# Turning a segment's result on VectorE instead of TensorE, with the weights' rows dealt out by eights, and three edits around it

## The chip, the cores and the metric

The kernel runs on one core of one Trainium2 chip. The metric is the device time of one execution in microseconds (us); lower is better. Engines are named as in the profile: PE (TensorE; PEld its weight loads), DVE (VectorE), ACT (ScalarE), POOL (GpSimd), SP (SyncE, which here only issues DMAs). ACTq, POOLq and SPq are the issues of DMAs on those engines.

## What is computed

Two independent heads whose outputs stand side by side.

Head A is attention with a recurrent memory. x is [2048, 1024], cut into 64 segments of 32 rows; the memory has 8 rows; there are 32 heads of width 128, and all weights are bf16:

```python
mem = mem0
for s in range(64):
    h = concatenate([mem, x[32*s:32*s+32]])          # 40 rows of 1024
    q, k, v = h @ Wq, h @ Wk, h @ Wv                 # 1024 -> 32 heads x 128
    p = softmax(mask(q @ k.T * 128**-0.5))
    o = (p @ v) @ Wo                                 # 4096 -> 1024
    mem = o[:8]                                      # goes into the next segment
    out_a[32*s:32*s+32] = o[8:]
```

The memory rows make the 64 segments a chain: no segment's projections can be finished before the result of the one before is there.

Head B is a long convolution per channel: K[d, l] = Re(sum over n of C dt B exp(dt A l)) for 1024 channels, 128 states and 2048 steps, then y = irfft(rfft(u) rfft(K)) + u D.

## The kernel before

**Part B comes first** (`part_b`, up to about 700 us). It builds tables, computes the filter and its spectrum by matmuls with sine matrices (MF), and multiplies and transforms back. What part A can have ahead of time runs beside it: `Ahead.transposes` turns x (L107), `Ahead.projections` computes q, k and v of the last 8 rows of each segment for all segments (L167) and leaves them in DRAM as PKd (keys, queries) and VXd (values, and the turned x). The last stage of part B is a loop over 16 blocks b. In it `load_k` fetches rows of the filter (KT from Kd, L1008) by many small DMAs, collected in `keys` and sent ten per block; `load_inverse` fetches u into uu (L1247); `spectrum` and `inverses` are PE work; `pointwise` is DVE work; L1306 and L1307 multiply and add u on DVE; the result is stored from ACT's queue (L1308). `load_inverse` runs NIV = 3 inverses ahead in 2 x NIV = 6 buffers. In the same loop `resident` loads part A's weights (L229) on SyncE, in the order of the program, into space that part B gives up.

**Part A** (`part_a`) keeps most of the weights in SBUF as blocks of [128, 2048], keyed (matrix, half, kc): kc is one of the eight groups of 128 rows of the 1024, and group kc holds rows 128 kc to 128 kc + 127. Twelve blocks a segment have no place and are streamed from DRAM copies (WD_k, WD_q, WD_v, WD_o, 512 KB each) through four slots, wst w0 to w3 (L297, SyncE): a slot is loaded again once PE has used it. Three more blocks (`KEPT`) stay in PSUM as raw words: `load_kept` puts them there, and `fetch` copies them on DVE (L292) into the arena, a small area of SBUF with fixed offsets (`AT`), each time they are needed. Of two of them (`HALF`) one half stays in SBUF instead, loaded a second time from DRAM.

The instruction order of each engine is the order of the program (`manual_schedule`). A segment goes through: k of half 0 (`quads`, L365, eight blocks of four concurrent 32-column matmuls of 512), q of half 0, k of half 1; then `put_kl` (L379, POOL) copies the early keys from the tile pk, which `load_pk` fetched from PKd on ACT's queue (L327) at the end of the segment before; scores (L390, L394); q of half 1, v, softmax on DVE and ACT, p v (L444), and the output projection (`oproj`, L475) into pp[:, 1, :], a [128, 256] f32 tile in PSUM: partition 32 qt + r holds row r, columns 256 qt to 256 qt + 255.

Then the result is turned, since the next segment needs its memory rows as columns of hT [128, 8, 32] (row group on the partitions, then kc, then row). This is the end of a segment:

```python
for j in range(2):                                               # ACT, L568
    nc.scalar.copy(out=osb[:, 128*j:128*j+128], in_=pp[:, 1, 128*j:128*j+128])
pv_l(pl[:], 1, V1, L1)                                           # PE
for j in range(2): nc.tensor.transpose(out=pt_o[j], in_=osb[...])   # PE, L574
for j in range(2): nc.vector.tensor_copy(out=hT[:, :, XM:SL]..., in_=pt_o[j]...)  # DVE, L576
fetch(("k", 0, 7))                                               # DVE, L292, five pieces
nc.scalar.copy(out=ob[:, 1, 0:128], in_=pp[:, 0, 0:128])         # ACT, L579
pk = load_pk(s + 1)                                              # ACT's queue, L327
nc.scalar.copy(out=ob[:, 1, 128:256], in_=pl[:]...)              # ACT, L582
stores(s, ob)                                                    # ACT's queue, L343 and L347
```

The first copy of hT holds the even row groups, the second the odd ones, and so the next k of half 0 goes through the groups as 0, 2, 4, 6, 1, 3, 5, 7. Group 7 is the one that `fetch` unpacks. osb is ob[:, 0, :].

Of the kernel before, what the change touches and what calls it, by code (L numbers as in the profile page):

```python
# [10 lines left out]
BF16 = mybir.dt.bfloat16  # L11
F32 = mybir.dt.float32
# [20 lines left out]
SLOTS = 4  # L33
# [6 lines left out]


def weight_blocks(Wq, Wk, Wv, Wo):
    W3 = {"k": Wk.rearrange("(kc p) he -> kc p he", p=128),
          "q": Wq.rearrange("(kc p) he -> kc p he", p=128),
          "v": Wv.rearrange("(kc p) he -> kc p he", p=128)}
    WoU = Wo.rearrange("(u h e) d -> u e h d", h=2, e=128)

    def src(key):
        if isinstance(key, str):
            return W3[key]  # L50
        if key[0] == "o":
            return WoU[key[1]]
        m, t, kc = key
        return W3[m][kc][:, t * 2048:(t + 1) * 2048]
    return src
# [18 lines left out]
class Ahead:  # L74
# [18 lines left out]
    def transposes(self, pool, ps, ident):  # L93
        nc = self.nc
        def load(b):
            xb = pool.tile([128, self.Dm], BF16, name="xb", tag="xb")
            nc.gpsimd.dma_start(out=xb[:], in_=self.x[b * 128:(b + 1) * 128, :])
            return xb
        xbs = [load(b) for b in range(3)]
        yield  # L100
        for b in range(self.S // 128):
            if b + 3 < self.S // 128:
                xbs.append(load(b + 3))
            xb = xbs[b]
            pt = ps.tile([128, self.KC, 4, self.SL], BF16, name="pt_x", tag="ptx")
            for kc in range(self.KC):
                nc.tensor.transpose(out=pt[:, kc, :, :].rearrange("p a b -> p (a b)"), in_=xb[:, kc * 128:(kc + 1) * 128], identity=ident[:])  # L107
            yield
            xst = pool.tile([128, 4, self.KC, self.XM], BF16, name="xst", tag="xst")
            nc.scalar.copy(out=xst[:].rearrange("p s k r -> p k s r"), in_=pt[:, :, :, 0:self.XM])  # L110
            nc.scalar.copy(out=self.xTl[:, :, 4 * b:4 * b + 4, :], in_=pt[:, :, :, self.XM:self.SL])  # L111
            nc.sync.dma_start(out=self.VXd[4 * b:4 * b + 4, :, 256:].rearrange("s p f -> p s f"), in_=xst[:].rearrange("p s k r -> p s (k r)"))
            yield
# [119 lines left out]
def part_a(ctx, tc, x, src, WD, HE, seg_len, out_a, ahead, W_res, rest, places, first):  # L233
    nc = tc.nc
    S, Dm = x.shape
    M = 8
    SL = seg_len
    E = 128
    KC = Dm // 128
    NS = S // SL  # L240
    assert SL == 32 and M == 8 and Dm == 1024 and HE == 4096
    XM = 24
# [5 lines left out]
    ident, mask, BD, BDx, BDL, hT = ahead.consts  # L248
# [4 lines left out]
    wst = ahead.wst  # L253
    wres = ctx_w.enter_context(tc.tile_pool(name="a_wres", bufs=1, side="right"))

    loads = [SLOTS]
# [20 lines left out]
    ps = ctx_l.enter_context(tc.tile_pool(name="a_ps", bufs=1, space=PSUM))  # L277
    ps_k = ctx_l.enter_context(tc.tile_pool(name="a_keep", bufs=1, space=PSUM))
    kept, ahead_of, halves = {}, {}, {}
# [11 lines left out]
    def words(out, in_):  # L291
        nc.vector.tensor_scalar(out=out.bitcast(I32), in0=in_.bitcast(I32), scalar1=0, scalar2=None, op0=ALU.bitwise_or)  # L292

    def stage(key, in_):
        t_ = wst.tile([128, 2048], BF16, name="wst", tag="w%d" % (loads[0] % SLOTS))
        loads[0] += 1
        nc.sync.dma_start(out=t_[:].rearrange("e (h d) -> e h d", h=2) if len(in_.shape) == 3 else t_[:], in_=in_)  # L297
        return t_

    def load_kept(key):  # L300
        t_ = first.pop(key) if key in first else stage(key, src(key))
        kept[key] = {}
        for n in (1,) if key in HALF else (0, 1):
            kept[key][n] = ps_k.tile([128, 512], F32, name="keep", tag="keep%d" % sum(len(b) for b in kept.values()))
            words(kept[key][n][:], t_[:, 1024 * n:1024 * n + 1024])
        if key in HALF:
            t_ = ahead.low["half"] if key[0] == "q" else wres.tile([128, 1024], BF16, name="Whalf")
            nc.sync.dma_start(out=t_[:], in_=src(key)[:, 0, :] if key[0] == "o" else src(key)[:, 0:1024])
            halves[key] = [(0, 1024, t_)]

    def fetch(key):

# [44 lines left out]
    for s in range(NS):  # L357
        def quads(m, t, kcs, a=None):
            if a is None:
                a = ps.tile([128, 512], F32, name="acc", tag=BANK[m, t])  # L360
            for kc in kcs:
                w = unit((m, t, kc))
                for g in range(4):
                    for o_, rhs in columns(w, 512 * g, 512):
                        nc.tensor.matmul(a[32 * g:32 * g + 32, o_:o_ + rhs.shape[1]], lhsT=hT[:, kc, :], rhs=rhs,  # L365
                                         start=(kc == 0), stop=(kc == KC - 1), tile_position=(0, 32 * g), skip_group_check=True)
            return a
# [107 lines left out]
                            nc.tensor.matmul(po[32 * qt:32 * qt + 32, o_:o_ + rhs.shape[1]], lhsT=oT[:, h % 4, (h % 16) // 4, :], rhs=rhs,  # L475
                                             start=False, stop=(h == 31), tile_position=(0, 32 * qt), skip_group_check=True)

        a = quads("k", 0, (0, 2, 4, 6, 1, 3, 5, 7))
        k0 = evac(a, "k0")
        a = quads("q", 0, range(0, 6))  # L480
        fetch(("q", 0, 7))
# [82 lines left out]
        oproj(pp[:, 1, :], (8, 10, 12, 14, 9, 11, 13, 15), o1)  # L564
        ob = at("ob", 2, 256)
        osb = ob[:, 0, :]
        for j in range(2):
            nc.scalar.copy(out=osb[:, 128 * j:128 * j + 128], in_=pp[:, 1, 128 * j:128 * j + 128])  # L568
        pl = ps.tile([128, 4, 32], F32, name="pl", tag="b2")
        pv_l(pl[:], 1, V1, L1)  # L570
        if s + 1 < NS:
            pt_o = [ps.tile([128, 4, SL], BF16, name="tro", tag=tag) for tag in ("b0", "b1")]
            for j in range(2):
                nc.tensor.transpose(out=pt_o[j][:].rearrange("p a b -> p (a b)"), in_=osb[:, 128 * j:128 * j + 128], identity=ident[:])  # L574
            for j in range(2):
                nc.vector.tensor_copy(out=hT[:, :, XM:SL].rearrange("p (q j) r -> p j q r", j=2)[:, j], in_=pt_o[j][:, :, XM:SL])  # L576
        if s + 1 < NS:
            fetch(("k", 0, 7))
        nc.scalar.copy(out=ob[:, 1, 0:128], in_=pp[:, 0, 0:128])  # L579
# [67 lines left out]
def part_b(ctx, tc, u, A_re, A_im, B_re, B_im, C_re, C_im, log_dt, Dskip, out_b, ahead, copies, residents, first_state):  # L647
    nc = tc.nc
# [36 lines left out]
    with tc.tile_pool(name="b_par", bufs=1) as par, tc.tile_pool(name="b_parh", bufs=2) as parh, tc.tile_pool(name="b_mg", bufs=2) as mg, \  # L685
# [84 lines left out]
        o = 0  # L770
# [467 lines left out]
        for j, op in ((0, ALU.add), (1, ALU.subtract)):  # L1238
            v.tensor_tensor(out=Bt[:, kc, j], in0=Y[:, 0], in1=Y[:, 1], op=op)

    NIV = 3
    unsent = []

    def load_inverse(dq, c):
        r, mc = c // 4, c % 4
        uu = iv.tile([128, 2, DQ], BF16, name="uu", tag="uu", bufs=2 * NIV)
        sy.dma_start(out=uu[:], in_=u_v[r][:, mc:mc + 2, DQ * dq:DQ * dq + DQ])  # L1247
        return uu

# [70 lines left out]
    for b in range(16):  # L1320
        dq = b // 4
        if b % 4 == 0:
            Bs[dq] = (bp0, bp)[dq % 2].tile([128, 4, 2, 2, 2, DQ], BF16, name="Bt", tag="B")
        if b == 0:
            ks += [load_k(DQ * i, DQ, (sy,), KT2[i - 2], keys) for i in (2, 3)]
        if b == 3:
            nxt = [load_inverse(*todo[n_]) for n_ in range(NIV)]
            pointwise(b, *now)
            ctx_h.close()
            ctx_p.close()  # L1330
            ps_h = ctx.enter_context(tc.tile_pool(name="b_psh", bufs=3, space=PSUM))
            ps_y = ctx.enter_context(tc.tile_pool(name="b_psy", bufs=2, space=PSUM))
        if b + 1 < 16:
            s_ = [ps_h.tile([128, 2, 2, DQ], F32, name="hps", tag="h") for _ in range(2)]
            spectrum(b + 1, [halves(t_) for t_ in s_])
            then = s_[0][:], odd([halves(t_) for t_ in s_])
        if b != 3:
            pointwise(b, *now)
        now = then
        if b + 2 < 16:  # L1340
            spectra.append(load_u(b + 2))
        for _ in range(min(10, len(keys))):
            keys.pop(0)()
        if b < 4:
            for i in (2 * b, 2 * b + 1):
                sy.dma_start(out=MI[i][:], in_=MId[2 * i:2 * i + 2].rearrange("c p a k q -> p c a k q"))
        for _ in range({1: 1, 2: 1, 3: 1, 6: 4, 11: 2, 12: 2, 13: 4, 14: 4}.get(b, 0)):
            next(resident)
        if b == 4:
            state = first_state(iv.tile([8, D], BF16, name="m0", bufs=1), iv.tile([128, 8, 24], BF16, name="xt0", bufs=1))  # L1350
            next(state)
        if b == 13:
            state.send(ps_y.tile([128, 8, 128], BF16, name="yp", tag="yp")[:, :, 0:8])
        if b >= 4:
            inverses(2)
        if b == 6:
            negate(ks[1:])
# [38 lines left out]
def kernel(  # L1396
# [78 lines left out]
    def first_state(m0, xt):  # L1475
        nc = tc.nc
        hT = constants(tc, ahead)
        nc.sync.dma_start(out=xt[:].rearrange("p k r -> p (k r)"), in_=ahead.VXd[0, :, 256:])
        nc.sync.dma_start(out=m0[:], in_=A_mem0[0])
        pm = yield  # L1480
        for kc in range(8):
            nc.tensor.transpose(out=pm[:, kc, :], in_=m0[:, kc * 128:(kc + 1) * 128], identity=ahead.consts[0][0:8, 0:8])
        nc.vector.tensor_copy(out=hT[:, :, ahead.XM:], in_=pm)
        nc.gpsimd.tensor_copy(out=hT[:, :, 0:ahead.XM], in_=xt[:])
        yield
# [40 lines left out]
```

## Time and profile before

| | |
|---|---|
| median of 3 runs | 2073.23 us (2067.98 to 2073.27) |
| the profiled execution | 2060.34 us, of which the span from first to last instruction is 2058.6 |
| mean granted PE clock | 0.982 |
| part A, first to last of 64 segments | L579 runs from 749.0 to 1998.7 us |
| last matmuls of part A (L611) | from 1998.55 us, 55 us |
| DMA | 590.78 MB, 287 GB/s on the mean |
| streamed blocks | 256 + 192 + 192 + 128 = 768 DMAs of 512 KB |

How to read it: PE's busy time is modelled for pipelined matmuls. A "wait" line gives who waited, for what, the total in us, how often, and the longest. A timeline line gives the start and length in us, the engine, the line of the kernel, the operation, output and input, and in brackets the idle time of the engine before it with what ended it. In the chain of waits each row is what the end waited on at that time. In the 40 slices each digit is a busy share in tenths of 51.5 us.

### The profile page before, as it was taken

To read this page: it belongs to the slowest core of one execution; us is meant where nothing else is said; L and a number is where in the kernel's file an instruction comes from. 1 tells how busy PE (TensorE), PEld (TensorE's weight loads), DVE (VectorE), ACT (ScalarE), POOL (GpSimd) and SP (SyncE) were. 2 spreads that over 40 slices of the span, in tenths; PEclk is the share of its full clock that TensorE was granted. 3 is DMA by queue.
4 is the path that set the end of the run, shared out by engine and by line. 5 is a ranking of instruction groups with operands and counts; after the bars stand their busy time and mean duration, and the time that the engine had idled before them with its cause. 6 is when DMAs were issued, how large, how long until landed. Compare 5 with 4: busy or idle time off the path is not lost.

```text
span 2058.6 us, 78592 instructions
## 1 busy us (share of the span) xinstructions
PE 1875.7 (91%) x33734; PEld 1190.4 (58%) x33734; DVE 1416.1 (69%) x3352; ACT 1051.5 (51%) x1981; POOL 379.8 (18%) x748
## 2 busy tenths in 40 slices
PE   2699999977999779999999999999999999999999
PEld 1365666656888535555555555555555555555554
DVE  8689989989899346666656656666566666666650
ACT  5899999961333234444444444444444444444430
POOL 2133343353000011111111111111111111111121
PEclk9999999989999879999999999999999999999999
DMA  7697986565736899999999999999999999999991
GB/s 192 177 255 213 261 229 180 157 207 184 228 123 206 311 330 340 341 342 344 344 334 340 340 339 339 347 333 334 338 340 354 344 343 347 339 331 350 333 341 52
DMA packets 351186, 590.78 MB, mean 287 GB/s; under 512 B 108536, under 2 KB 228376, under 8 KB 348788
## 3 DMA queue, kind: packets, MB, share of 16 engines
q1 hardware_dynamic: 297016, 528.00, 75.6%
q10 hardware_dynamic: 44812, 28.26, 4.4%
q0 software_dynamic: 9008, 29.49, 4.3%
q8 instruction: 264, 4.33, 0.8%
q14 instruction: 86, 0.70, 0.1%
HBM read 530.86 MB, written 65.26 MB: 290 GB/s over the span
## 4 chain that ended last, share of the span: by engine, by line
PE 35%; DMA 17%; DVE 1%; issue 1%; ACT 1%; POOL 0%; ACTq 0%; POOLq 0%; DVEq 0%
PE acc L365 20%; PE pp L475 7%; DMA wst<-WD_v 4%; DMA wst<-WD_o 4%; DMA wst<-WD_q 3%; PE pe L611 3%; DMA wst<-WD_k 3%; DMA arena<-PKd 2%; PE tr L376 2%; PE pv L444 1%; DMA out_dram<-arena 1%; PE sc L390 1%; PE pv L448 1%; ACT arena L568 0%; PE sc L394 0%
## 5 line engine op out<-in xcount | busy, mean ns | idle before, releaser
L365 PEld LDWEIGHTS <-a_hT 128*32 128x32 bf16 x12352 | 338.6, 96 | 305.9 <-issue 59.2
L371 ACT CAST arena<-acc 128x512 bf16<-128x512 f32 x384 | 225.1, 586 | 377.0 <-PE acc L365 315.9
L365 PE MATMUL acc<-W,a_hT 128*32 128x512 bf16 x4608 | 375.8, 383 | 0.8 <-issue 0.7
L475 PEld LDWEIGHTS <-arena 128*32 128x32 bf16 x8256 | 212.1, 97 | 93.9 <-issue 45.3
L365 PE MATMUL acc<-wst,a_hT 128*32 128x512 bf16 x2304 | 234.1, 383 | 19.2 <-DMA wst<-WD_v 10.0
L292 DVE TENSOR_SCALAR arena<-keep 128x256 int32<-128x256 int32 (+1 forms) x512 | 176.4, 396 | 42.1 <-PE acc L365 38.0
L379 POOL COPY arena<-arena 128x128 bf16<-128x128 bf16 x128 | 37.6, 294 | 854.1 <-DMA arena<-PKd 316.5
L365 PE MATMUL acc<-MF,a_hT 128*32 128x512 bf16 x2048 | 172.6, 384 | 0.0
L475 PE MATMUL pp<-W_o,arena 128*32 128x256 bf16 x4096 | 138.2, 275 | 7.7 <-DMA W_o<-in_A_Wo_dram 6.3
L414 DVE TENSOR_REDUCE a_mx<-sc 128x4 f32<-128x160 f32 (+1 forms) x192 | 73.1, 381 | 81.8 <-ACT sc L410 81.8
L406 DVE TENSOR_REDUCE a_mx<-sc 128x4 f32<-128x160 f32 (+1 forms) x192 | 72.0, 375 | 82.3 <-PE sc L394 80.6
L167 PE MATMUL pro<-xTl,wsl 128*128 128x512 bf16 x512 | 119.0, 383 | 9.5 <-ACT xTl L111 5.0
L410 ACT ACTIVATE sc<-sc 128x160 f32<-128x160 f32 (+1 forms) x192 | 63.9, 333 | 120.6 <-DVE sc L407 101.3
L1060 PEld LDWEIGHTS <-MF 128*128 128x128 bf16 x1024 | 102.6, 101 | 30.2 <-issue 8.7
L490 DVE COPY arena<-tr 128x512 bf16<-128x512 bf16 x64 | 27.2, 425 | 130.7 <-PE tr L376 130.7
L437 POOL TENSOR_TENSOR arena<-arena,a_BD 128x128 bf16<-128x128 bf16 x128 | 71.1, 555 | 240.1 <-DVE arena L424 221.0
L1060 PE MATMUL hps<-KT,MF 128*128 128x256 bf16 x720 | 94.6, 284 | 14.4 <-DVE x L1229 11.3
L461 ACT CAST arena<-pv 128x256 bf16<-128x256 f32 (+1 forms) x192 | 79.1, 449 | 49.0 <-PE pp L444 39.1
L1287 PE MATMUL yp<-Bt,MI 128*128 128x256 bf16 x680 | 102.9, 273 | 0.8 <-ACT yb L1303 0.8
L568 ACT CAST arena<-pp 128x128 bf16<-128x128 f32 x128 | 27.8, 269 | 141.7 <-PE pp L475 141.7
L1098 ACT ACTIVATE E<-pa 128x648 bf16<-128x648 f32 x128 | 91.4, 714 | 16.9 <-PE pa L1090 9.4
L365 PE MATMUL acc<-W_v,a_hT 128*32 128x512 bf16 x1280 | 93.7, 382 | 0.9 <-issue 0.8
(313 smaller groups left out, 3966.6 us busy)
## 6 DMA issues: line engine op xcount, KB each, us to landing
wst<-WD_v SPq DMA_DIRECT2D x256, 512.0 KB
wst<-WD_k SPq DMA_DIRECT2D x192, 512.0 KB
wst<-WD_o SPq DMA_DIRECT2D x192, 512.0 KB
wst<-WD_q SPq DMA_DIRECT2D x128, 512.0 KB
Ud<-ux POOLq DMA_DIRECT2D x16, 1024.0 KB, 5.5
uq<-Ud SPq DMA_DIRECT2D x32, 512.0 KB
wsl<-in_A_Wk_dram SPq DMA_DIRECT2D x16, 512.0 KB
wsl<-in_A_Wv_dram SPq DMA_DIRECT2D x16, 512.0 KB
```

The costliest lines, as they stand in the source:

```text
L167: nc.tensor.matmul(a[:], lhsT=w[:, kc, 128 * j:128 * j + 128], rhs=xTl[:, kc, :, :].rearrange("p s k -> p (s k)"), start=(kc == 0), stop=( ...
L292: nc.vector.tensor_scalar(out=out.bitcast(I32), in0=in_.bitcast(I32), scalar1=0, scalar2=None, op0=ALU.bitwise_or)
L365: nc.tensor.matmul(a[32 * g:32 * g + 32, o_:o_ + rhs.shape[1]], lhsT=hT[:, kc, :], rhs=rhs, start=(kc == 0), stop=(kc == KC - 1), tile_pos ...
L371: nc.scalar.copy(out=q, in_=a[:])
L406: nc.vector.tensor_reduce(out=m_, in_=x, axis=AX.X, op=ALU.max)
L414: nc.vector.tensor_reduce(out=m_, in_=x, axis=AX.X, op=ALU.add)
L437: nc.gpsimd.tensor_tensor(out=L[:, 0].rearrange("p (a b) k -> p a b k", a=4), in0=bc(lt[:, :, 0:XL].unsqueeze(2), [128, 4, 4, XL]), in1=bc ...
L461: nc.scalar.copy(out=o[:, i:i + n], in_=p[:, i:i + n, :].rearrange("p a (g q) -> p a g q", g=4))
L475: nc.tensor.matmul(po[32 * qt:32 * qt + 32, o_:o_ + rhs.shape[1]], lhsT=oT[:, h % 4, (h % 16) // 4, :], rhs=rhs, start=False, stop=(h == 3 ...
L1060: pe.matmul(s_[r][half][:, cs, :], lhsT=MF[:, kc, 4 * rr + mc, cs, :], rhs=rhs, start=(i == 0 and mc == 0), stop=(i == 1 and mc == 3), ski ...
L1098: sc.activation(out=T["E", r, e // 4][:, lo:lo + 8 * NE].rearrange("p (i c) -> p i c", i=2), in_=T.pop(("p", r, e))[:, :, 0:4 * NE], func= ...
L1287: pe.matmul(yp[:, b, :], lhsT=m_[:, b, cs, kc, :], rhs=Bt[:, kc, j, half, c_, :], start=(kc == 0 and cs == 0 and half == 0), stop=(kc == 3 ...
```

## The change

- The result is turned by DVE. Two block transposes (32 x 32, f32 words) read pp from PSUM with a stride of eight words and write hm, an f32 tile; two copies put the eight memory rows into hT as bf16. The first pair serves row groups 0 and 1, the second 2 to 7. hm lies in the arena at ob's offset and has ob's whole size, so osb's copy on ACT comes after it, now as one copy of 256. The two PE transposes, their PSUM tiles and the two DVE copies are gone.
- A block transpose leaves element (row r, column 8 d + k) of a 256-column group on partition d of block k. So group k now holds the rows k, 8 + k, 16 + k, ...: the weight blocks are cut from Wk, Wq and Wv by "(p kc)" instead of "(kc p)", and x and mem0 are turned with the same stride. Within a block each row is still one run of 2048 values. k of half 0 goes through the groups in order 0 to 7.
- The loads of KT for the second half of the channels are issued from SyncE and GpSimd in turn, twelve per block of the loop instead of ten.
- u is loaded six inverses ahead, in nine buffers.
- `load_kept` loads each half of a half-kept block once, one half into a slot and the other into its place.

```diff
 def weight_blocks(Wq, Wk, Wv, Wo):
-    W3 = {"k": Wk.rearrange("(kc p) he -> kc p he", p=128),
+    W3 = {"k": Wk.rearrange("(p kc) he -> kc p he", p=128),
...
-                nc.tensor.transpose(out=pt[:, kc, :, :].rearrange("p a b -> p (a b)"), in_=xb[:, kc * 128:(kc + 1) * 128], identity=ident[:])
+                nc.tensor.transpose(out=pt[:, kc, :, :].rearrange("p a b -> p (a b)"), in_=xb[:].rearrange("r (p k) -> r k p", p=128)[:, kc, :], identity=ident[:])
...
     def load_kept(key):
-        t_ = first.pop(key) if key in first else stage(key, src(key))
         kept[key] = {}
         for n in (1,) if key in HALF else (0, 1):
             kept[key][n] = ps_k.tile([128, 512], F32, name="keep", tag="keep%d" % sum(len(b) for b in kept.values()))
-            words(kept[key][n][:], t_[:, 1024 * n:1024 * n + 1024])
         if key in HALF:
-            t_ = ahead.low["half"] if key[0] == "q" else wres.tile([128, 1024], BF16, name="Whalf")
-            nc.sync.dma_start(out=t_[:], in_=src(key)[:, 0, :] if key[0] == "o" else src(key)[:, 0:1024])
-            halves[key] = [(0, 1024, t_)]
+            w = wst.tile([128, 2048], BF16, name="wst", tag="w%d" % (loads[0] % SLOTS))
+            loads[0] += 1
+            h_ = ahead.low["half"] if key[0] == "q" else wres.tile([128, 1024], BF16, name="Whalf")
+            for n, t_ in ((1, w[:, 0:1024]), (0, h_[:])):
+                nc.sync.dma_start(out=t_, in_=src(key)[:, n, :] if key[0] == "o" else src(key)[:, 1024 * n:1024 * n + 1024])
+            words(kept[key][1][:], w[:, 0:1024])
+            halves[key] = [(0, 1024, h_)]
+        else:
+            t_ = first.pop(key)
+            for n in (0, 1):
+                words(kept[key][n][:], t_[:, 1024 * n:1024 * n + 1024])
...
-        a = quads("k", 0, (0, 2, 4, 6, 1, 3, 5, 7))
+        a = quads("k", 0, range(KC))
...
         ob = at("ob", 2, 256)
         osb = ob[:, 0, :]
-        for j in range(2):
-            nc.scalar.copy(out=osb[:, 128 * j:128 * j + 128], in_=pp[:, 1, 128 * j:128 * j + 128])
+        if s + 1 < NS:
+            hm = at("ob", 512).bitcast(F32).rearrange("p (k r) -> p k r", r=SL)
+            for k in (slice(0, 2), slice(2, KC)):
+                nc.vector.transpose(out=hm[:, k, :], in_=pp[:, 1, :].rearrange("p (d k) -> p k d", k=KC)[:, k, :])
+                nc.vector.tensor_copy(out=hT[:, k, XM:SL], in_=hm[:, k, XM:SL])
         pl = ps.tile([128, 4, 32], F32, name="pl", tag="b2")
         pv_l(pl[:], 1, V1, L1)
-        if s + 1 < NS:
-            pt_o = [ps.tile([128, 4, SL], BF16, name="tro", tag=tag) for tag in ("b0", "b1")]
-            for j in range(2):
-                nc.tensor.transpose(out=pt_o[j][:].rearrange("p a b -> p (a b)"), in_=osb[:, 128 * j:128 * j + 128], identity=ident[:])
-            for j in range(2):
-                nc.vector.tensor_copy(out=hT[:, :, XM:SL].rearrange("p (q j) r -> p j q r", j=2)[:, j], in_=pt_o[j][:, :, XM:SL])
+        nc.scalar.copy(out=osb, in_=pp[:, 1, :])
         if s + 1 < NS:
             fetch(("k", 0, 7))
         nc.scalar.copy(out=ob[:, 1, 0:128], in_=pp[:, 0, 0:128])
...
-    NIV = 3
+    NIV, UU = 6, 9
...
-        uu = iv.tile([128, 2, DQ], BF16, name="uu", tag="uu", bufs=2 * NIV)
+        uu = iv.tile([128, 2, DQ], BF16, name="uu", tag="uu", bufs=UU)
...
-            ks += [load_k(DQ * i, DQ, (sy,), KT2[i - 2], keys) for i in (2, 3)]
+            ks += [load_k(DQ * i, DQ, (sy, gp), KT2[i - 2], keys) for i in (2, 3)]
...
-        for _ in range(min(10, len(keys))):
+        for _ in range(min(12, len(keys))):
             keys.pop(0)()
```

More of the change, by code (lines that the diff above doesn't have):

```diff
@@ L42, in weight_blocks @@
 def weight_blocks(Wq, Wk, Wv, Wo):
-    W3 = {"k": Wk.rearrange("(kc p) he -> kc p he", p=128),
-          "q": Wq.rearrange("(kc p) he -> kc p he", p=128),
-          "v": Wv.rearrange("(kc p) he -> kc p he", p=128)}
+    W3 = {"k": Wk.rearrange("(p kc) he -> kc p he", p=128),
+          "q": Wq.rearrange("(p kc) he -> kc p he", p=128),
+          "v": Wv.rearrange("(p kc) he -> kc p he", p=128)}
     WoU = Wo.rearrange("(u h e) d -> u e h d", h=2, e=128)
@@ L1481, in first_state @@
         for kc in range(8):
-            nc.tensor.transpose(out=pm[:, kc, :], in_=m0[:, kc * 128:(kc + 1) * 128], identity=ahead.consts[0][0:8, 0:8])
+            nc.tensor.transpose(out=pm[:, kc, :], in_=m0[:].rearrange("r (p k) -> r k p", p=128)[:, kc, :], identity=ahead.consts[0][0:8, 0:8])
         nc.vector.tensor_copy(out=hT[:, :, ahead.XM:], in_=pm)
```

## The prediction

> **What bounds the kernel now.** I began with the page's busy shares and its 40 slices, to find the stages.
>
> ```profile
> PE 1875.7 (91%) x33734; PEld 1190.4 (58%) x33734; DVE 1416.1 (69%) x3352; ACT 1051.5 (51%) x1981; POOL 379.8 (18%) x748
> PE   2699999977999779999999999999999999999999
> DMA  7697986565736899999999999999999999999991
> ```
>
> From slice 15 on, PE and the DMA engines both read 9: that is part A, 64 segments. L579 runs once in each, from 749.0 to 1998.7 us, so a segment takes 1249.7 / 63 = 19.84 us and 0.1 us in each is worth 6.3 us. Next, the windows (length; PE, PEld, DVE, ACT, POOL busy; clock, DMA share, GB/s):
>
> ```profile
> 680.00:700.00 20.00, 18.18 (x173) 15.64 (x177) 2.04 (x5) 8.76 (x14) 0.00 (x0) 1.00 0.94 343
> 700.00:720.00 20.00, 11.68 (x142) 5.44 (x133) 7.82 (x19) 3.60 (x8) 0.30 (x1) 0.66 0.86 291
> 720.00:748.00 28.00, 16.54 (x268) 7.84 (x264) 9.04 (x28) 6.53 (x13) 2.54 (x6) 0.68 1.00 367
> 1300.00:1500.00 200.00, 190.60 (x4254) 110.83 (x4253) 124.61 (x391) 89.72 (x210) 28.58 (x70) 1.00 0.95 337
> ```
>
> In steady state PE has 95% and DMA 95%: neither has much room, and a microsecond taken from one need not shorten the segment. The hand-over between the parts (700 to 748) is a DMA stage with PE half idle. Third, the waits of 900 to 1900 us, some 51 segments: POOL's line and PE's two largest.
>
> ```profile
> POOL arena L379 <- DMA arena<-PKd: 256.0, 38, 7.6
> PE acc L365 <- DMA wst<-WD_v: 5.7, 10, 1.3
> PE pp L475 <- DMA wst<-WD_o: 4.7, 10, 0.8
> ```
>
> All PE waits there add up to 23 us, 0.45 a segment, 17 of them for streamed blocks. POOL waits for the PKd load in 38 segments; the chain that ended last shows who needs it:
>
> ```profile
> 1403.73 0.03 ACT arena L568
> 1403.76 0.04 issue
> 1403.79 6.68 DMA arena<-PKd
> ...
> 1410.90 0.30 POOL arena L379
> 1411.20 0.04 issue
> 1411.25 0.28 PE sc L390 x16
> ```
>
> The scores start 0.35 us after POOL starts to copy, so this load, issued at a segment's end, ends on PE's path. Last, one segment's end in the timeline:
>
> ```profile
> 1444.12 0.27 ACT L568 CAST arena<-pp 128x128 bf16<-128x128 f32 x1 [2.30 <-PE pp L475]
> 1444.19 0.33 ACTq L327 DMA_DIRECT2D arena<-PKd  x1
> ...
> 1444.71 0.34 DVE L576 COPY a_hT<-tro 128x32 bf16<-128x32 bf16 x2 [0.89 <-PE tro L574]
> ...
> 1444.94 0.40 PE L365 MATMUL acc<-Wlow,a_hT 128*32 128x512 bf16 x4
> 1444.99 1.35 DVE L292 TENSOR_SCALAR arena<-keep 128x256 int32<-128x256 int32 x4
> ...
> 1446.26 0.22 DVE L292 TENSOR_SCALAR a_S<-keep 128x64 int32<-128x64 int32 x1
> ```
>
> The projection ends at 1444.10; k0 starts 0.84 later, and PKd is issued only 0.09 after the end: ACT's sequencer passes the copies without waiting for them. DVE then needs until 1446.48 to unpack key block 7, which PE takes at 1446.46 to 1446.64.
>
> **Part 1, the turn.** Removed: copy, two transposes on PE, two DVE copies, 0.84 us. Added on DVE: transposes of 64 and 192 words from PSUM, copies of 16 and 48. No row turns 32-bit words. From below, L424 and L423 (bf16 in SBUF) give 0.20 for 64 and, between 0.31 for 128 and 0.45 for 256, 0.38 for 192; from above, twice that, since a word is twice as wide. L292 reads 256 words from PSUM every 0.335 us, full pace for a word, so I take the lower end. Copies: 0.17 as L576. With 0.06 a step between dependent ones, the first two blocks of hT stand at 0.02 + 0.20 + 0.06 + 0.17 = 0.45 us, the rest at about 1.05 (1.6 if doubled). A k0 block takes 0.215: two run from 0.49 to 0.92, the third waits to 1.09, q0 could start at 1.09 + 6 x 0.215 = 2.38. But L292's five pieces (1.49 us in the trace) now start at about 1.0 and end at 2.5, so q0 starts at 2.5 to 2.6; before, at 1446.68 - 1444.10 = 2.58. Gain: 0 to 0.1 us (loss 0.5 if doubled). The unpacking is late next.
>
> **Part 2, what the turn does to ACT's queue.** hm lies in ob's bytes. The copy of the result to osb therefore waits for DVE's last copy, 1.05 us, and behind it on ACT are queued the pp copy, the PKd issue, the pl copy and both stores. PKd is issued near 1.15 instead of 0.09: 1.06 later (1.6 if doubled). POOL's copy started 5.5 us after the end in this segment (1449.57) and 7.15 in the one of the chain (1410.90); the median over the segments in the trace's records is 6.2. A later issue meets a stream that has drained somewhat; the spread of landings suggests up to 0.4 back. So POOL starts near 6.2 + 1.06 - 0.4 = 6.85, the scores near 7.2, where PE without that wait reaches them at 1450.59 - 1444.10 = 6.5: 0.7 exposed, about 0.1 to 0.15 so far, so 0.55 to 0.6 more. While PE stands, SyncE's blocks go on landing, so of PE's 0.45 a segment some 0.3 comes back. Net +0.25 us, x 63 = +15.8. Ends: -0.1 (all refunded, turn 0.1 faster; -6) and +1.06 (nothing refunded; +67).
>
> **Part 3, u six ahead.** Three DVE waits:
>
> ```profile
> DVE uu L1306 <- DMA uu<-in_B_u_dram: 23.2, 3, 8.6
> PEld L365 <- DVE arena L292: 6.8, 1, 6.8
> PE yp L1287 <- ACT mn L1255: 5.6, 3, 2.4
> ```
>
> The first (6.74, at 536.90) stood behind an 11.47 us run of ten KT loads on SyncE; it reached PE as 2.4 us through ACT. Take -2.4 (0 to -6.7). The other two, 8.6 and 7.8, hold DVE until 704 and so the unpacking of key block 7, for which PE stands 6.8 us. They go; next is DMA, which at 367 GB/s can only give back its idle time: 6% of 20, 14% of 20, 3.9 us (0 to -6.8). The buffers' lag is unchanged (9 - 6 = 6 - 3), so SyncE waits for stores as before, but fewer times at the end.
>
> **Part 4, the small edits.** Half-kept blocks once: 0.52 MB less in that stage, at 367 GB/s -1.4 (0 if PE is late). KT loads shared: SyncE's turn per block falls from ten to six; GpSimd pays 0.6 each (L974, three in 1.83) with POOL 18% busy, and its constants move behind them but are needed only at 645: 0; if POOL were late, the negation of KN, now waiting 1.6, would wait on. Rows by eights leaves packet sizes as they are; whether the wider stride slows the one-time loads no row shows: 0, up to +5. The strided weight loads of L107 (147 ns) precede matmuls that wait 41 us for xb: 0, up to +5. Key block order moves streamed block 2 from second to third: 0.2 us more grace, in Part 2's refund.
>
> A rule that speaks against Part 4: the Trainium skill, "DMA: Bandwidth & Descriptors", Rules for kernel authors, says that spreading DMAs over the issuing engines does not help bandwidth and only saves sequencer time. The trace agrees that nothing there is short of bandwidth (DMA 0.71 in 520 to 540) while the issue run is what delayed u. By the rule alone the sharing is worth 0, as I have it; by the row it could be part of the 2.4, already counted.
>
> **Sum.** +15.8 - 2.4 - 3.9 - 1.4 = +8.1 on the profiled execution's 2060.3 us. The runs' median, 2073.2, lies 12.9 above that execution; I add the difference to the median: 2081.3. About 0.3% (6 us) is what a measurement of this kernel tells from no change.
>
> **Rivals.**
> *The stream sets the pace.* DMA is at 0.95 and 17 of 23 us of PE's waits are for blocks; if a wait at the scores only replaces such waits (0.45 a segment is there to be replaced), Part 2 costs nothing, and Part 1 gives 0.05 x 63 = 3: 2073.2 - 2.4 - 3.9 - 1.4 - 3 = 2062. It decides when the load lands less than about 0.5 us later than now. Against: POOL's 38 waits. Chance 0.40.
> *Nothing drains.* The landing moves by the full 1.06 and only 0.3 returns: +0.65 x 63 = 41, 2106. Chance 0.10.
> *The turn is not shorter.* If 32-bit transposes cost double, k0 ends 0.5 later, inside PE's wait, and PKd 1.6: 1.0 more exposed, less the whole 0.45, 0.55 x 63 = 35, 2100. No row excludes it. Chance 0.08.
> *Forecast* 2081, own range 2070 to 2096: 0.42.
>
> Faster by over 0.3%: 0.36 of the first rival. Same: 0.04 of it and 0.16 of the forecast, 0.20. Slower: 0.26 + 0.10 + 0.08 = 0.44. The range runs from 2055 (first rival with 7 more in Part 3) to 2104; outside are the two upper rivals' upper halves and the unlikely full bounds.
>
> **What would show it.** L576's transposes from PSUM near 0.2 and 0.38 us (wrong if doubled); k0 starting near 0.5 after the projection's end but q0 no earlier than 2.5; the PKd issue near 1.15; POOL's L379 start near 6.9 and PE waiting for it; fewer PE waits for WD blocks; no uu wait; segment 0 ending 5 to 8 us sooner. A segment of 19.8 or less with PKd late would make the forecast wrong and the first rival right.

## The result, and the profile after

The changed kernel takes 2081.86 us (median of 21 runs, 2074.41 to 2092.02), the kernel before 2071.89 us (21 runs, 2057.52 to 2084.58): 10.0 us slower by the medians. The ratio, which is not taken from the medians, is 1.0067, 95% interval 1.0049 to 1.0084: 10 to 17 us. The profiled execution took 2074.41 us, its span is 2072.7 (before: 2058.6); it is the fastest of the 21. Lines below the diff have moved: L365 is now L371, POOL's copy of the keys L379 is L385, the scores L390 are L396, the projection L475 is L481, the PKd load L327 is L333. The turn is L576 and L577, the result's copy L580.

The page's busy shares and DMA slices:

```profile
PE 1859.7 (90%) x33608; PEld 1198.1 (58%) x33608; DVE 1446.9 (70%) x3478; ACT 1048.4 (51%) x1917; POOL 398.8 (19%) x778
DMA  7686986567636999999999999999999999999991
```

PE does 16 us less (1875.7 to 1859.7) and DVE 31 more, while the time grew: PE stands longer. The windows of the hand-over and of the steady state (length; PE, PEld, DVE, ACT, POOL busy; clock, DMA share, GB/s):

```profile
680.00:700.00 20.00, 18.54 (x188) 14.91 (x189) 6.14 (x16) 7.56 (x15) 0.00 (x0) 1.00 1.03 369
700.00:720.00 20.00, 14.66 (x259) 7.07 (x252) 9.78 (x26) 8.12 (x15) 2.07 (x5) 0.91 0.88 313
1300.00:1500.00 200.00, 188.12 (x4258) 113.30 (x4246) 130.69 (x412) 89.24 (x201) 28.44 (x70) 1.00 0.96 337
```

Ahead of part A time was won: PE has 14.66 us of work from 700 to 720 instead of 11.68, and the first segment ends at 738.6 instead of 748.6 us (end of the projection's matmuls). In part A more than that was lost: from there to the last segment's end it is 1273.7 us instead of 1249.7, or 20.22 a segment instead of 19.84. The waits from 900 to 1900 us say where (us in total, times, longest):

```profile
POOL arena L385 <- DMA arena<-PKd: 318.0, 43, 9.0
ACT arena L580 <- DVE a_hT L577: 153.8, 49, 4.1
PE sc L396 <- POOL arena L385: 28.2, 34, 2.3
PE acc L371 <- DMA wst<-WD_k: 7.0, 12, 1.2
```

ACT now waits for the last copy of the turn in every segment, POOL for PKd in 43 instead of 38, and PE for POOL at the scores in 34, 0.57 us a segment on the mean of some 50. Before, in the same window:

```profile
PE sc L390 <- POOL arena L379: 0.2, 1, 0.2
```

PE's waits for streamed blocks did not shrink: all four kinds of them add up to 20.0 us against 17.0. The chain that ended last runs through all three:

```profile
1404.72 0.20 DVE a_hT L577
...
1404.99 0.07 ACT arena L580
...
1405.10 5.46 DMA arena<-PKd
...
1410.70 0.30 POOL arena L385
...
1411.04 0.28 PE sc L396 x16
```

And one segment's end in the timeline; the projection ended at 1443.99:

```profile
1444.02 0.25 DVE L576 STREAM_TRANSPOSE arena<-pp 128x64 f32<-128x64 f32 x1 [0.31 <-PE pp L481]
1444.31 0.18 DVE L577 CAST a_hT<-arena 128x16 bf16<-128x16 f32 x1
1444.39 0.38 DVE L576 STREAM_TRANSPOSE arena<-pp 128x192 f32<-128x192 f32 x1
1444.54 0.61 PE L371 MATMUL acc<-Wlow,a_hT 128*32 128x512 bf16 x8 [0.29 <-DVE a_hT L577]
1444.80 0.19 DVE L577 CAST a_hT<-arena 128x48 bf16<-128x48 f32 x1
1445.08 0.37 ACT L580 CAST arena<-pp 128x256 bf16<-128x256 f32 x1 [3.01 <-DVE a_hT L577]
1445.18 0.33 ACTq L333 DMA_DIRECT2D arena<-PKd  x1
```

The turn takes 0.97 us, k0 starts 0.55 us after the projection's end, and the PKd issue, behind ACT's copy, 1.19 after it.

### The profile page after: what moved, and what is told of

Same layout as the page of the kernel before. It is cut to its first block, busy times and chain, and to the rows that moved or that the text cites. A ratio compares the mean times of both kernels' runs of the same rounds, so it can differ in the third digit from the quotient of the medians.

```text
span 2072.7 us, 78480 instructions
## 1 busy us (share of the span) xinstructions
PE 1859.7 (90%) x33608; PEld 1198.1 (58%) x33608; DVE 1446.9 (70%) x3478; ACT 1048.4 (51%) x1917; POOL 398.8 (19%) x778
## 5 line engine op out<-in xcount | busy, mean ns | idle before, releaser
L371 PEld LDWEIGHTS <-a_hT 128*32 128x32 bf16 x12352 | 358.6, 96 | 289.6 <-DVE a_hT L577 50.1
L371 PE MATMUL acc<-W,a_hT 128*32 128x512 bf16 x4608 | 376.3, 381 | 0.3 <-issue 0.3
L481 PEld LDWEIGHTS <-arena 128*32 128x32 bf16 x8256 | 211.1, 97 | 98.9 <-issue 44.7
L371 PE MATMUL acc<-wst,a_hT 128*32 128x512 bf16 x2304 | 237.5, 382 | 16.6 <-DMA wst<-WD_k 7.2
L385 POOL COPY arena<-arena 128x128 bf16<-128x128 bf16 x128 | 37.3, 292 | 878.8 <-DMA arena<-PKd 390.9
L371 PE MATMUL acc<-MF,a_hT 128*32 128x512 bf16 x2048 | 177.5, 382 | 0.0
L481 PE MATMUL pp<-W_o,arena 128*32 128x256 bf16 x4096 | 138.3, 275 | 7.2 <-DMA W_o<-in_A_Wo_dram 5.6
L580 ACT CAST arena<-pp 128x256 bf16<-128x256 f32 x64 | 23.8, 372 | 209.1 <-DVE a_hT L577 204.1
L371 PE MATMUL acc<-W_v,a_hT 128*32 128x512 bf16 x1280 | 93.2, 380 | 2.3 <-issue 2.3
```

## The experiments

Theory: the loss in part A is the later PKd issue and nothing else of the turn. Rivals: the stream of blocks sets the pace, so that PKd does not matter; or the turn itself costs time. The table has for each kernel the median, the ratio to the kernel before with its interval, and from the traced execution the time of the PKd issue and of the first scores after the projection's end and the length of a segment (issue: median; scores, segment: mean, from the fourth segment on). Differences to the kernel before are taken to its runs beside the kernel in question, whose median was 2071.0, 2069.1 or 2067.3 us. A segment's length is that of one execution: the seven kernels whose part A has neither the turn nor a late load range from 19.80 to 20.03, so a difference of 0.1 says nothing and one of 0.2 little.

| kernel | us | ratio to before | issue | scores | segment |
|---|---|---|---|---|---|
| before | 2071.9 | 1 | 0.10 | 6.87 | 19.80 |
| the change | 2081.9 | 1.0067 [1.0049, 1.0084] | 1.20 | 7.36 | 20.20 |
| change, PKd load first | 2058.4 | 0.9929 [0.9907, 0.9950] | -0.11 | 6.71 | 19.88 |
| the turn alone | 2094.7 | 1.0104 [1.0083, 1.0124] | 1.20 | 7.58 | 20.42 |
| all but the turn | 2059.1 | 0.9941 [0.9915, 0.9966] | 0.10 | 6.90 | 19.89 |
| all but the turn, PKd load first | 2059.4 | 0.9949 [0.9928, 0.9971] | -0.11 | 6.88 | 19.90 |
| before, PKd load last | 2166.5 | 1.0426 [1.0382, 1.0470] | 1.87 | 8.34 | 21.19 |
| before, PKd load after pl's copy | 2070.8 | 0.9996 [0.9971, 1.0021] | 0.36 | 6.92 | 19.93 |
| change, hm apart | 2067.0 | 0.9993 [0.9969, 1.0016] | 1.03 | 7.24 | 20.10 |
| change, PKd load first, a block fewer | 2034.6 | 0.9841 [0.9808, 0.9873] | -0.11 | 6.69 | 19.69 |
| change, a block fewer | 2070.3 | 0.9996 [0.9971, 1.0022] | 1.22 | 7.47 | 20.21 |
| u alone | 2067.9 | 0.9991 [0.9970, 1.0011] | 0.10 | 6.85 | 19.91 |
| key loads alone | 2060.0 | 0.9956 [0.9935, 0.9977] | 0.10 | 6.84 | 19.91 |
| half-kept blocks alone | 2068.9 | 0.9994 [0.9973, 1.0014] | 0.10 | 6.84 | 20.03 |

**The change with the PKd load ahead of the turn.**

```diff
         oproj(pp[:, 1, :], (8, 10, 12, 14, 9, 11, 13, 15), o1)
+        if s + 1 < NS:
+            pk = load_pk(s + 1)
         ob = at("ob", 2, 256)
...
-        if s + 1 < NS:
-            pk = load_pk(s + 1)
```

> The changed kernel with one line moved: the PKd load is issued on ACT ahead of the turn, so it does not stand behind the copy that waits for hm. Theory (the later PKd issue is the whole loss of part A, 24.0 us in 63 segments): the issue falls from 1.19 us after the projection's end to before 0.1, POOL's L385 copy starts near 6.2 or sooner instead of 6.8, segments of 19.8 instead of 20.2, and the hand-over keeps its 10 us: 2081.9 - 24 = 2058, 0.7% below the kernel before. Rival 1 (the stream of blocks sets the pace and PKd is only where PE happens to wait): segments stay at 20.2, PE's waits for WD blocks grow by what the wait at the scores loses, 2080 to 2084. Rival 2 (the turn on VectorE is itself the cost: later unpacking of the kept words, key block order): the same 2080 to 2084, but with the scores early and k0 or q0 late.

2058.4 us, the theory's number: the loss is gone, 23.5 us by the medians, 22.6 by each kernel's distance from the runs of before beside it, and the kernel beats the one before. The turn, the key order and the copy's wait are all still there; only the load has moved. PE's wait for POOL at the scores is nearly gone (900 to 1900 us of this kernel):

```profile
PE sc L396 <- POOL arena L385: 0.8, 2, 0.4
```

Its waits for WD_v blocks rose from 4.5 to 13.1, so the first rival was right about one thing: with PKd early, the blocks are what comes last.

**The turn alone**, on the kernel before.

> The kernel before with the turn alone (rows by eights, VectorE's transposes, key block order), without the edits of u, of the key loads and of the half-kept blocks. Theory (parts add up): only the part A loss, +24 us, 2071.9 + 24 = 2096, the first segment ending where it did before (748.6 within 2 us). Rival (the edits ahead of part A change how part A runs, by their memory or by what is loaded): the segments are back at 19.8 and the time is within 6 us of 2072.

2094.7, 23.7 above its kernel before. The theory's numbers held: the first segment ends at 747.5 (748.6 before), and the loss is in part A. The wait at the scores, in the waits from 900 to 1900 of this kernel:

```profile
PE sc L390 <- POOL arena L379: 37.6, 41, 3.2
```

**All but the turn**, on the kernel before.

> The kernel before with everything but the turn: u six ahead in nine tiles, key loads of SyncE and GpSimd, half-kept blocks loaded once. Theory (parts add up): the first segment ends 10 us sooner, segments stay at 19.8, 2071.9 - 10 = 2062. Rival (the gain before part A is lost in part A, or came from the rows by eights): within 3 us of 2072.

2059.1, 11.9 less, and the two halves add up: 23.7 - 11.9 = 11.8, where the whole change measured 10.0. The first segment ends at 743.6 us, 5 us sooner than in the trace before and not 10, but 8 and 11 sooner than in the two kernels below that move only the load and do the same work as before up to there (751.9 and 754.3): a single trace does not give this gain to better than some us.

**The kernel before with the PKd load after the stores.**

```diff
         nc.scalar.copy(out=ob[:, 1, 0:128], in_=pp[:, 0, 0:128])
-        if s + 1 < NS:
-            pk = load_pk(s + 1)
         nc.scalar.copy(out=ob[:, 1, 128:256], in_=pl[:].rearrange("p a k -> p (a k)"))
         if s + 1 < NS:
             stores(s, ob)
+            pk = load_pk(s + 1)
```

> The kernel before with one line moved: the PKd load is issued by ACT after the two stores of the segment, nothing else changed. Theory (issue time of PKd is passed on to the segment): the issue moves from 0.1 to some 1.5 to 2.5 us after the projection's end; the change's 1.1 us gave 0.38 a segment, so 0.5 to 0.9 a segment, +32 to +57 us, 2104 to 2129, with POOL's copy starting past 7.0 and PE's wait at the scores for POOL. Rival 1 (the stream sets the pace): 2069 to 2075, with fewer waits for WD blocks. Rival 2 (the turn is the cost): the same 2069 to 2075.

2166.5: the direction is the theory's, but 95 us is far over its 32 to 57. I had scaled the loss with the issue time; it does not go in proportion. The issue came 1.77 us later, the scores 1.47, the segment 1.39. PE's wait for POOL at the scores is 68.6 us from 900 to 1900.

**The kernel before with the PKd load after pl's copy**, ahead of the stores.

> The kernel before with the PKd load one place further back on ACT: after the copy of pl, ahead of the two stores (behind them it was issued at 1.87 and cost 95 us). pl is ready 0.4 to 0.5 us after the projection's end, so the issue should fall near 0.6 to 0.8. Theory (the issue time decides, nothing at 0.1 or sooner, 0.40 us a segment at 1.2, 1.39 at 1.87): 0.1 to 0.25 us a segment, +6 to +16 us, 2077 to 2087. Rival 1 (there is 0.5 us of grace before it costs anything): 2068 to 2074. Rival 2 (in the other experiment the stores ahead of it in ACT's queue were the cost, not the time): the same 2068 to 2074, and then the change's 24 us at 1.2 had another source than the issue time.

The issue moved less than I had thought, to 0.36 instead of 0.6 to 0.8, and the time did not move: rival 1, a grace, holds at least that far. Whether it reaches 0.5 is open, and so is whether the two stores ahead of the load made the last kernel worse than the time alone; no run had a load at 1.87 without them.

**The change with hm apart**, to take away the wait and leave the order.

```diff
-            hm = at("ob", 512).bitcast(F32).rearrange("p (k r) -> p k r", r=SL)
+            hm = at("o1", 512).bitcast(F32).rearrange("p (k r) -> p k r", r=SL)
```

> The changed kernel with one word changed: hm lies in the bytes of o1, free once the projection has read it, and no longer in ob's. So ACT's copy of the result waits for nothing on VectorE and the order of all instructions is as in the change. Theory (that wait, through the PKd issue behind it, is the whole loss of part A): the issue falls from 1.20 to near 0.1 us after the projection's end, POOL's L385 starts near 6.2, segments of 19.8 to 19.9, 2056 to 2062, as with the load moved ahead of the turn (2058.4). Rival 1 (the load has to be ahead of the turn, as there, at -0.5): 2065 to 2072. Rival 2 (ACT and VectorE now read the same PSUM at once, and the turn stretches past 1.2 us): k0 starts later than 0.8 and the time is above 2070.

The theory's number failed, because the edit does not do what I wrote. ACT still waits, now for the second transpose instead of the last copy:

```profile
ACT arena L580 <- DVE arena L576: 143.2, 49, 4.1
```

The issue came only 0.17 us sooner, at 1.03. The shared bytes were half the reason for the wait; what the copy and that transpose still share is pp, which both read, but that this is why the wait stands is read from the program, and no run took it away. The 12 to 15 us that this brought (by distances from before, or by the medians) are more than the 0.10 us a segment of the traced executions, 6 us. Much of that is which execution was traced: that of the change lies 7.5 us below its median, this one 3.6 above. The time lies in rival 1's range, but does not speak for it, since the load is still late. (Single issues of the first experiment come at -0.5; their median is -0.11.)

**A streamed block fewer**, with PKd first and with PKd late.

```diff
     def unit(key):
+        if key == ("v", 1, 4):
+            key = ("v", 1, 3)
```

> The changed kernel with the PKd load ahead of the turn (the first experiment), and with one streamed block fewer in each segment: the weights' block v 1 4 is replaced by the resident block v 1 3, so the output is another one; PE's work stays the same. A block is 0.52 of the 6.7 MB that a segment moves at 337 GB/s, 1.5 us of the DMA engines' 19.0. Theory (with PKd early the stream of blocks is the pace, which is why the 0.28 us that the turn saves PE gave nothing): the segment falls from 19.88 until PE's 18.8 us and its own waits hold it, to 19.1 to 19.4: 30 to 48 us less than 2058, 2010 to 2028, with PE's waits for WD blocks below 10 us in 900 to 1900. Rival (PE's chain of waits sets the pace, the DMA share of 0.955 is just where it ends up): 2050 to 2060, the DMA share down to 0.88.

> The changed kernel as it is (PKd late, at 1.2 us), with the same streamed block replaced by the resident one (another output). Against the experiment before it says what the late load costs when the stream has 1.4 us to spare in a segment. Theory (a wait of PE at the scores is lost for good; the stream can't give it back): the load lands sooner beside a lighter stream, but PE's wait remains the difference, 0.25 to 0.5 us a segment, 16 to 32 us above the experiment before, and about 30 us below the change. Rival (a stream with slack delivers PKd in time or catches up): within 6 us of the experiment before.

Of the 1.5 us of DMA that are gone from each segment only 24 us came back in the first, 0.38 a segment, short of the theory's 30 and well past the rival's 8. PE's waits for streamed blocks from 900 to 1900 fell from 26.9 to 12.1 us (I had expected less than 10), the DMA share from 0.95 to 0.91. So with PKd early the stream holds part of the pace; that PE's own chain is close behind it is argued from the rest, which no run tested. With PKd late the same relief brought 11.6 us instead of about 30, and the price of lateness rose from 23 to 35.7 us, over my 32. A stream with time to spare (DMA share 0.89, PE's waits for blocks 1.1 us) does not pay the late load back. The wait of the second kernel, 2.9 us in the first:

```profile
PE sc L398 <- POOL arena L387: 40.2, 47, 2.4
```

**u six ahead alone.**

> The kernel before with u six ahead in nine tiles alone. Theory (u is most of the 12 us that the edits ahead of part A brought: the first matmul of part A stands at 699, 703, 707 and 705 us in the four traced kernels that load u three ahead, at 693 to 696 in the six that load it six ahead, a mean difference of 9 us): 2070 - 8 to 10 = 2060 to 2062, no DVE wait for a uu load over 1 us from 500 to 760, part A starting near 695. Rival 1 (my first sum: 2.4 at 537 and 3.9 at the hand-over, 6.3): 2064. Rival 2 (the key loads of GpSimd made the gain; ten of SyncE's were what delayed u): 2068 to 2072, with a uu wait left at 537.

No gain: 2067.9 against 2067.3 of the runs beside it. I had set the six kernels with u six ahead against the four without, but the first six had the shared key loads as well. The late u is gone there, and PE stands all the same, for the keys; part A starts at 703.7 us (waits from 525 to 560 of this kernel):

```profile
ACT KN L1046 <- DMA KT<-Kd: 11.9, 2, 7.2
PE hps L1060 <- ACT KN L1046: 3.4, 1, 3.4
```

**Key loads of SyncE and GpSimd alone.**

> The kernel before with the key loads of SyncE and GpSimd alone, twelve to a block in place of ten, u three ahead. Theory (they bring nothing of their own when u is late for want of a tile ahead): 2066 to 2073. Rival (SyncE's run of key loads, 11.47 us for ten, was the cause of the late u at 537; half as many of its issues let u through): the uu wait at 537 gone and 2060 to 2065.

The rival was right: 2060.0, 7.3 us less. PE is busy without a gap from 530 to 560. (Two queues and twelve to a block were changed together; no run takes them apart.) The window in the kernel before, in the one with the PKd load after pl's copy, with u alone and with the key loads alone:

```profile
530.00:560.00 30.00, 27.63 (x254) 24.53 (x252) 22.70 (x25) 12.22 (x19) 0.35 (x1) 1.00 0.74 226
530.00:560.00 30.00, 23.32 (x191) 19.69 (x190) 18.76 (x22) 9.87 (x14) 0.35 (x1) 0.89 0.69 215
530.00:560.00 30.00, 26.44 (x226) 22.59 (x223) 28.96 (x31) 9.22 (x13) 0.92 (x1) 0.94 0.71 213
530.00:560.00 30.00, 30.00 (x277) 26.90 (x275) 27.98 (x33) 13.18 (x22) 0.00 (x0) 1.00 0.65 213
```

The second kernel is the same as the first up to part A. So the execution from which I predicted was a mild one: PE stood 2.4 us in this window, in the other 6.7, and there the mean granted clock is 0.89 as well.

**The half-kept blocks alone.**

> The kernel before with the half-kept blocks loaded once alone: 0.52 MB less at the hand-over. Theory: 1.4 us at 367 GB/s, 2067 to 2070. Rival (the hand-over is held by PE's wait for the unpacking of key block 7, not by bytes): 0, 2069 to 2071, which five rounds can hardly tell from 1.4; a gain of 4 or more would be a surprise and would say that bytes set the hand-over.

0.9994, not to be told from nothing or from 1.4 us.

**All but the turn, with the PKd load first**, at the place of the first experiment.

> The kernel before with the edits ahead of part A, without the turn, and with the PKd load ahead of the copies of the result: the same place as in the first experiment, so that the two differ by the turn alone. Theory (with PKd early the stream of blocks and its four slots hold the segment, and the 0.28 us of k0's earlier start is not passed on): within 5 us of 2058.4, 2054 to 2063. Rival 1 (the turn costs something of its own, hidden there by the earlier load): 2045 to 2053. Rival 2 (the turn is worth its 0.28 us a segment, hidden nowhere): 2066 to 2076.

2059.4 against 2058.4 with the turn: the turn by itself is worth nothing that can be measured, either way. The edit does one thing more than the text on record says: the issue, 0.33 us on ACT's queue, now stands ahead of the copies of the result, and k0 starts 1.08 us after the projection's end instead of 0.85. So k0 is 0.5 us later here than with the turn, and even that is not passed on. The earlier load without the turn brings nothing over 2059.1. The kernel with the turn and the early load has the lowest median of those that stream every block, but the three at 2058 to 2059 (and the key loads alone, 2060.0) can't be told apart.

## Why the prediction was right, and where it was not

The sum was +8.1 us and +10.0 were measured by the medians (10 to 17 by the ratio's interval). Two terms were off, part A's cost by 6 to 8 us and the gain ahead of it by 4, in opposite directions; that the sum came so close is partly luck.

**Part 1, the turn: right.** The transposes took 0.25 and 0.38 us (I took 0.20 and 0.38), not double; k0 starts at 0.55 instead of 0.85 after the projection's end (medians). That k0's end would not move because the unpacking is late next is shown: the unpacking ends 2.41 us after the projection's end (2.39 before), PE takes its last piece 0.08 us later, and ACT's copy of k0 begins at 2.99, against 2.97 before.

**Part 2, the PKd issue: the mechanism right, one term too small.** Issue 1.20 (near 1.15), POOL's copy at 6.94 (6.85), scores at 7.36 (near 7.2), PE waiting there for POOL 0.57 us a segment (0.55 to 0.6 more than before). The size of that wait is right with some luck: the scores came 0.16 later than I had them, but PE also reaches them later than at 6.5, which was one segment's time; before, they start at 6.87 with next to no wait (0.2 us in all, not 0.1 to 0.15 in each). The term that was mis-sized is the refund, "of PE's 0.45 a segment some 0.3 comes back". The eight traced kernels with the issue at 0.36 or earlier have their scores at 6.85 and segments of 19.91 on the mean. Against that the four with a late load and the full stream (the change, the turn alone, hm apart, PKd last) have the scores 0.51, 0.73, 0.39 and 1.49 later and segments 0.29, 0.51, 0.19 and 1.28 longer: each time about 0.2 came back, whatever the delay. That figure is rough: against the changed kernel with the load first (6.71, 19.88) the three with the turn give back 0.3. By the medians the cost is 22 to 24 us, 0.35 to 0.38 a segment, instead of 15.8, 0.25. A possible reason for such a ceiling, argued and not shown, is that the stream runs ahead by four slots only. While PE stands it frees none, and SyncE's queue waits for PE; the largest such group from 900 to 1900 before, in the change and with the load after the stores:

```profile
SPq L297 <- PE acc L365: 311.6, 353, 1.7
SPq L297 <- PE acc L371: 359.0, 347, 2.3
SPq L297 <- PE acc L365: 422.2, 330, 7.5
```

The total grows with PE's stand at the scores (it is 313.5 and 319.6 with the load at -0.11 and at 0.36). The longest single wait says less: it is 2.3 and 2.9 in those two kernels as well. By this reading "SyncE's blocks go on landing" is true until the slots are full. Against it stands the pair with a block fewer, where the stream has time to spare: scores 0.78 later, segments 0.52 longer, again about 0.25 back. More slots would test it; that wasn't tried, and the cause of the small refund stays open.

**Parts 3 and 4: the sum too small, and put on the wrong edit.** 11.9 us instead of 7.7. I gave u 6.3 and the shared key loads 0; measured alone, the key loads brought 7.3 and u 0.6 the other way by the medians (by the ratio's interval between 6 us of gain and 2 of loss). The step that failed is that loading u six ahead makes PE's stand go with u's waits: the cause stood in the same paragraph, SyncE's 11.47 us run of ten loads. With u moved ahead in that queue, the keys are late instead. The words of the Trainium skill, "DMA: Bandwidth & Descriptors", Rules for kernel authors, that spreading over issuing engines only saves sequencer time, agree with the runs (213 GB/s in the window with either edit); I was wrong to read from it that the saving is worth 0 here: the run of issues was the bound. And the size came from one execution, which happened to lose 2.4 us where others lost more. The 3.9 us at the hand-over do not show: with the key loads alone, where DVE is still late there, the first segment ends at 743.9 us, with all but the turn at 743.6 and, with the load first as well, 741.3.

**The rivals.** "The stream sets the pace" (2062) failed for the load at 1.2 and is right up to 0.36, where a later issue costs nothing. "Nothing drains" (2106) failed: of 1.10 us of later issue 0.63 reached POOL. Doubled transposes (2100) did not occur.

## What to carry to other kernels

Before a step is moved to another engine, look at who reads or overwrites its buffers and what is queued behind that reader: here a turn that starts the next work sooner cost 23 us because a DMA issue stood behind a copy that had come to wait, and moving one line ahead of it gave all of it back. Do not count on a busy stream of loads to pay a stall back: here some 0.2 us came back of stalls of 0.4 to 1.5 us, and the rest of the wait was paid. When a load is late behind a run of issues in one queue, loading it earlier in the same queue makes another load late; shorten the run.

## What was not expected of the hardware

With the weights' rows dealt out by eights, 4 KB packets that started between 120 and 400 us took 197 to 202 ns on the mean in all six kernels with that edit, and 216 to 227 in the eight without; I had allowed for the wider stride being slower, not faster. What this is worth to the time was not measured; the steady stream's packets, from copies laid out as before, took 181 and 182 in the two kernels compared (before and change).
